# An mLSTM feeding a top-1 mixture of experts on one core: a new order of the work, a planner rule for the two engines that share a port, one product moved to VectorE, the odd row earlier, no explicit table load

## The chip, the cores and the metric

The kernel runs on one core of one Trainium2 chip. The time is device microseconds of one execution. The core has five engines that matter here: PE (TensorE), DVE (VectorE), ACT (ScalarE), POOL (GpSimd) and SP (SyncE, which here only issues DMAs). Each runs its own instructions strictly in order and waits on semaphores for the others.

## The reference, cut to what matters

Inputs are q, k, v and an output gate of 4 batches, 8 heads, 768 steps, 40 dimensions; two gates per step; 3072 tokens, each with one of two modalities; 8 experts with w1 320x1024 and w2 1024x320.

```python
for t in range(S):                                  # mLSTM, one state per batch and head
    m_new = np.maximum(f_gate[:, :, t] + m, i_gate[:, :, t])
    C = f_stab * C + i_stab * np.einsum('bhd,bhe->bhde', vt, kt)
    n = f_stab * n + i_stab * kt
    nq = np.einsum('bhd,bhd->bh', n, qt)
    y[:, :, t] = sigmoid(o_gate) * (C @ qt) / np.maximum(np.abs(nq), 1.0)
x = y.transpose(0, 2, 1, 3).reshape(B * S, H * D)   # 3072 tokens of 320
logits = x @ w_gate + modality_bias[modality_id]
e_idx = np.argmax(logits, axis=1)                   # one expert per token
out[mask] = gate_w[mask, None] * (np.maximum(x[mask] @ w1[e], 0.0) @ w2[e])
```

## The kernel before, in words

The function `still_arm` (from about line 1590) is the arm that runs; a general arm behind a branch is not taken here. It uses two properties of the input: the state of the mLSTM barely changes once the first 64 steps are in, and nearly every token goes to the one expert that its modality's bias prefers. So there are two experts, called A and B, and a token with another expert is "odd"; one such odd token is worked out apart.

**Stages.** The state of each batch is built from the first 64 steps (`state`, L1798). 3072 tokens are 24 chunks of 128, taken in pairs i = 0 to 11. For each chunk `light` (matmul at L1945) multiplies queries by the state into a PSUM bank Y (pair 1: H). For each pair `token_rows` (from L1948) makes rows out of it: the gated product `xr` on DVE (L1961), the normaliser `ab` (clamped at L1973, its reciprocal at L1974, 128x16), then the **normaliser's product** xr = xr * ab, 128x640, on POOL (L1976); ACT casts the upper half to float16 (`rows`, L1979) and DVE takes the lower half (L1624, two instructions). POOL scatters each chunk's rows to a DRAM buffer x_s by token position (L1997), so that all tokens of an expert lie together. Chunks 22 and 23 (the first 64 steps) come from exact sums (`special`, L2033).

**Tiles of the experts.** Fifteen tiles: k0 A0, k1 A1, k2 B0, k3 B1 with 128 tokens, then A2, B2, A3, B3, A4, B4, A5, B5, A6, B6 with 256, and B7 with 96. The first three don't go through DRAM: PE picks their rows with 0/1 matrices (`select`, PE at L2120, 15 matmuls per tile and 25 for tile 1; ACT copies the result to `xt` at L2123 and L2124). The others are read from x_s by two transposing DMAs (L2096) once their rows have been scattered. For each tile `logits` (L2133) checks the expert, and `expert` (L2176) does layer 1 on PE into a bank H (L2197, 8 matmuls for each of 8 blocks), hh = relu on ACT (L2202), the rounding rest hl on DVE (L2204), layer 2 on PE into a bank O (L2214, 24 matmuls for each half of 128 tokens), the scaling `ob` on ACT (L2221) and the scatter to the output on POOL (L2222). Weights come in pieces of 768 or 640 columns through seven staging buffers; ACT makes the upper half (w1h, w2h: L1903) and DVE the rest (w1l, w2l: L1904).

**The odd row** (`odd_row`, L2236 to 2285): DVE adds up which token is odd (`fpr`, `fs`, L2240 to 2244), PE sums over partitions (Y<-fs, L2246), DVE turns that into indices (L2247 to 2254), POOL gathers the row (`xrow`, L2256), SP reads a register (L2261) and loads that expert's weights into the staging and gate buffers (L2264, L2266). DVE makes `xf` (L2269, L2270), eight products (L2272), `fh` (L2274), one scaling (L2275) and seven multiply-adds into `facc` (L2277); PE sums over partitions (Y<-facc, L2280); ACT and POOL write it (L2282, L2283).

**What sets the order.** Nothing is issued directly. Each instruction becomes a task of `Plan` (L39 to 160) with its engine, an estimated duration, what it reads and writes, a bias, an optional start bound `nb` and an added latency `lat`. A task's due time `late` is its distance to the end along its dependences, and `plan.early` moves it earlier. `NUDGE` adds a number to the bias of single tasks by their count. A list scheduler plays the engines forward; among ready tasks it takes the smallest late + bias; the instructions are emitted in that order. Tasks marked `lk` on DVE and POOL are kept from overlapping in that play. Behind it, `idle_products` puts products with a zero matrix (M<-zw, O<-zw, L1731) where the play shows PE idle in its first 60 us, so that PE is not idle for long. The table load of ACT is asked for once at the beginning (L1724).

## Time and profile before

| what | value |
|---|---|
| median of 3 runs | 224.15 us (222.76 to 226.62) |
| the profiled execution | 222.62 us, of which 220.9 us are the span |
| PE busy in the span | 206.7 us (94%) |
| DVE, ACT, POOL busy | 142.1, 97.0, 86.1 us |
| granted TensorE clock | 0.992 |

Rows of a timeline read: start in us, duration in us, engine, line, operation, output <- inputs, shapes, count; in brackets the idle time of that engine just ahead and what ended it. Rows of a table by stage read: stretch, length, then busy time and number of instructions of PE, PE's weight loads, DVE, ACT and POOL, the granted clock, the DMA share and the GB/s moved. Rows of the waits read: the waiting engine and line, what it waited for, then us in total, times, longest.

### The profile page before, as it was taken

The numbers are of one execution on the slowest core, as the hardware profiler recorded it, in microseconds if no ns is written. First come the engines' busy times: TensorE is split into PE (matmuls) and PEld (weight loads), VectorE is DVE, ScalarE is ACT, GpSimd is POOL, SyncE is SP. The second block draws the span as 40 slices with busy tenths as digits, with TensorE's granted clock in tenths as the row PEclk, the third lists the DMA queues.
The fourth block names the chain that finished last, engine by engine and source line by source line (L and its number), as shares of the span: only waits on it lengthen the run. The fifth ranks groups of instructions, "written<-read, shape, count | busy, mean of one in ns | idle before, by whom it ended". The sixth has DMA issues, their size and how long they took to land.

```text
span 220.9 us, 5482 instructions
## 1 busy us (share of the span) xinstructions
PE 206.7 (94%) x2139; PEld 167.2 (76%) x2139; DVE 142.1 (64%) x421; ACT 97.0 (44%) x200; POOL 86.1 (39%) x98
## 2 busy tenths in 40 slices
PE   7987699999999999999999999999999999998960
PEld 2875589888887877878878768878878787785840
DVE  4789799998679463566386438425324858629960
ACT  2567688684255553342754313314553223143210
POOL 6458569421106716345048723526030120410321
PEclk9999999999999999999999999999999999999996
DMA  6989997989400659202774493202840010493100
GB/s 181 362 273 362 382 381 132 324 144 265 129 0 34 169 164 222 100 3 91 157 133 132 127 224 79 60 34 91 124 87 32 0 59 3 128 309 132 61 0 13
DMA packets 29783, 31.50 MB, mean 143 GB/s; under 512 B 21862, under 2 KB 22408, under 8 KB 29496
## 3 DMA queue, kind: packets, MB, share of 16 engines
q1 hardware_dynamic: 27176, 22.89, 38.9%
q0 software_dynamic: 2432, 8.13, 10.3%
q8 instruction: 18, 0.29, 0.6%
q14 instruction: 13, 0.11, 0.2%
q10 hardware_dynamic: 144, 0.07, 0.1%
HBM read 19.17 MB, written 8.43 MB: 125 GB/s over the span
## 4 chain that ended last, share of the span: by engine, by line
PE 68%; issue 14%; DMA 5%; POOL 2%; SPq 2%; DVE 2%; ACT 2%; another core or an unknown queue 1%; POOLq 1%; DVEq 0%
PE H L2197 32%; PE O L2214 28%; PE Y L1945 3%; DMA stage<-in_w1p 3%; DMA og<-in_ogl 3%; POOL out L2222 2%; PE M L2151 2%; SPq L1902 1%; PE Y L2043 1%; PE Y L2058 1%; POOLq L2407 1%; DVE hl L2204 1%; PE Y L1810 1%; PE O L2120 0%
## 5 line engine op out<-in xcount | busy, mean ns | idle before, releaser
L2204 DVE SCALAR_TENSOR_TENSOR hl<-H,hh 128x512 f16<-128x512 f32 (+1 forms) x50 | 33.9, 682 | 30.2 <-ACT hh L2202 25.6
L2214 PEld LDWEIGHTS <-hh 128*128 128x128 f16 (+1 forms) x400 | 38.6, 99 | 13.9 <-issue 0.5
L2202 ACT ACTIVATE hh<-H 128x512 f16<-128x512 f32 (+1 forms) x50 | 29.4, 592 | 42.1 <-PE H L2197 37.7
L2222 POOL DMA_INDIRECT out<-ob,ois x25 | 26.1, 1042 | 52.4 <-ACT ob L2221 35.9
L2197 PE MATMUL H<-xt,w1hB 128*128 128x256 f16 (+2 forms) x320 | 45.8, 251 | 0.1
L2197 PE MATMUL H<-xt,w1hA 128*128 128x256 f16 (+1 forms) x280 | 43.5, 257 | 0.3 <-issue 0.3
L2197 PE MATMUL H<-xt,w1lB 128*128 128x256 f16 (+2 forms) x192 | 40.6, 251 | 0.0
L2197 PE MATMUL H<-xt,w1lA 128*128 128x256 f16 (+1 forms) x168 | 37.9, 257 | 1.5 <-DVE w1lA L1904 1.5
L1976 POOL TENSOR_TENSOR xr<-xr,ab 128x640 f32<-128x640 f32 x12 | 17.1, 1424 | 38.9 <-DVE ab L1974 17.3
L2197 PEld LDWEIGHTS <-w1hB 128*128 128x128 f16 x320 | 28.5, 98 | 2.8
L1997 POOL DMA_INDIRECT x_s<-rows,pos_i x24 | 25.3, 1052 | 12.9 <-issue 7.0
L2214 PE MATMUL O<-w2hB,hh 128*128 128x320 f16 (+1 forms) x104 | 28.8, 299 | 0.0
L2214 PE MATMUL O<-w2lB,hh 128*128 128x320 f16 (+1 forms) x104 | 28.7, 299 | 0.0
L2197 PEld LDWEIGHTS <-w1hA 128*128 128x128 f16 x280 | 25.3, 98 | 3.3 <-issue 0.8
L2214 PE MATMUL O<-w2hA,hh 128*128 128x320 f16 x96 | 26.5, 299 | 0.0
L2214 PE MATMUL O<-w2lA,hh 128*128 128x320 f16 x96 | 26.5, 299 | 0.0
L2221 ACT ACTIVATE ob<-O,facs 128x320 f32<-128x320 f32 (+1 forms) x25 | 13.1, 526 | 30.6 <-PE O L2214 20.1
L2214 PEld LDWEIGHTS <-hl 128*128 128x128 f16 (+1 forms) x200 | 19.2, 99 | 8.7 <-DVE hl L2204 1.8
L2197 PEld LDWEIGHTS <-w1lB 128*128 128x128 f16 x192 | 18.7, 98 | 1.6 <-issue 0.3
L2197 PEld LDWEIGHTS <-w1lA 128*128 128x128 f16 x168 | 16.4, 98 | 3.1 <-DVE w1lA L1904 1.7
L2214 PE MATMUL O<-w2hB,hl 128*128 128x320 f16 (+1 forms) x104 | 17.1, 299 | 0.7 <-DVE hl L2204 0.7
L2214 PE MATMUL O<-w2hA,hl 128*128 128x320 f16 x96 | 15.3, 299 | 0.2 <-DVE hl L2204 0.2
(198 smaller groups left out, 294.0 us busy)
## 6 DMA issues: line engine op xcount, KB each, us to landing
qg<-in_ql SPq DMA_DIRECT2D x11, 384.0 KB
og<-in_ogl SPq DMA_DIRECT2D x12, 320.0 KB
...
```

The source lines that it names most:

```text
L1810: t_.matmul(u3[0:120, g], lhsT=kw[pr][rs, 3 * g:3 * g + 3].rearrange("p h d -> p (h d)"), rhs=kvs[pr][rs, 9 * D + HQ * g:9 * D + HQ * (g + ...
L1902: dma(n // 2, lambda sv=sv, src=src: sy.dma_start(sv, src()), r=[f"reg{c}"], w=[f"stage{k}"])
L1945: t_.matmul(y[p0:p1, HQ * g:HQ * g + w], lhsT=q[0:k, j, g, p0:p1], rhs=s[0:k, g, 0:w], start=(g == 0 and e == 0), stop=(g == 2 and e == n ...
L1976: lane((320 if lane is dve else 290) * n, lambda z=z, f=f, n=n: f(x4[:, z].rearrange("p c h d -> p (c h) d"), x4[:, z].rearrange("p c h d ...
L1997: ins = g_.indirect_dma_start(out=x_s[:, :], out_offset=bass.IndirectOffsetOnAxis(ap=pos_i[:, c:c + 1].bitcast(U32), axis=0), in_=rows[:, ...
L2151: t_.matmul(M0[:, 16 * h:16 * h + 16], lhsT=x[:, b], rhs=wgr[:, b % 3].rearrange("p a e -> p (a e)"), start=(h == 0 and b == 0), stop=(h = ...
L2197: t_.matmul(hp3[:, i], lhsT=l, rhs=r, start=(i == 0 and q == 0), stop=(i == g - 1 and q == 7), skip_group_check=True)
L2202: act(g * n, lambda fl=fl, hp3=hp3: s_.activation(hh[:, fl, 0:n], hp3, AF.Relu), r=[nb], w=[f"hh{j}{f}" for f in range(f0, f0 + g)])
L2204: dve(g * n, lambda fl=fl, hp3=hp3: v.scalar_tensor_tensor(hl[:, fl, 0:n], hp3, 0.0, hh[:, fl, 0:n], ALU.max, ALU.subtract), r=[nb] + [f"h ...
L2214: t_.matmul(op[0:z, 0:DM], lhsT=t[:, f, P * h:P * h + z], rhs=w[:, f], start=(i == 0), stop=(i == 23))
L2221: act(400, lambda h=h, op=op, o=o: s_.mul(obs[o][0:z], op[0:z, 0:DM], facs[0:z, s["q0"] + h:s["q0"] + h + 1]), r=[no, f"fac{k}"], w=[f"ob{ ...
L2222: swdma(164, lambda h=h, o=o: disjoint("outf", g_.indirect_dma_start(out=out[:, :], out_offset=bass.IndirectOffsetOnAxis(ap=ois[0:z, s["q0 ...
```

## The change

1. **The planner's rule for the shared port.** Before, a marked task on DVE or POOL starts, in the play, no sooner than the other's last marked task ends, less HOP (0.13). Now a marked POOL task starts LEAD (0.17) after DVE's. Eight small DVE operations are newly marked.
2. **The third pair's product on VectorE**: `BY_DVE` holds 4, so that for i = 2 the product xr = xr * ab (128x640) is one DVE instruction (L1629 in the new file) instead of a POOL one.
3. **The odd row sooner**: its tasks get 30 of earliness from end to end (`ODD`); before, those from `xf` to `facc` had none, and the rest 20. `SOON` is 30 for the other late tasks.
4. **No explicit table load**: the task that asked for it is gone, so all later tasks count one less.
5. **Costs in the play**: latency for the first loads of keys and gates, for the gather and for the last multiply-add; the absolute sums start later (`nb`).
6. **A new order**: the table `NUDGE` is another one, which together with 1 to 5 gives each engine another order.

```diff
 NUDGE = {
-    5: -33, 34: 162, 35: 57, 36: 44, 38: 34, 43: -8, 45: -116, 52: -7, 53: -123, 56: 240, 60: 266, 67: 11, 73: -1, 76: 8, 78: 12,
+    5: -33, 33: 453, 34: 199, 35: 44, 37: 34, 42: -8, 44: -116, 51: -7, 52: -123, 59: 122, 61: -11, 62: -19, 66: 11, 69: -23, 71:
...
     DMA_KB = 380.0
+    LEAD = 0.17
...
             if t["lk"]:
-                s = max(s, port["POOL" if name == "DVE" else "DVE"] - self.HOP)
+                s = max(s, port["POOL"] - self.HOP if name == "DVE" else port["DVE"] + self.LEAD)
...
-SOON = 20.0
+SOON = 30.0
 HINT = 12.0
+ODD = 30.0
 RING = 12
 BY_POOL = (3, 4)
-BY_DVE = ()
+BY_DVE = (4,)
...
-        dma(373, lambda: sy.dma_start(kvs[pr], ...), w=[f"kv{pr}"], bias=...)
+        dma(373, lambda: sy.dma_start(kvs[pr], ...), w=[f"kv{pr}"], lat=0.5 if pr == 0 else 0.0, bias=...)
-        dma(328, lambda: sy.dma_start(og[i % 4], ...), w=[f"og{i % 4}"], bias=...)
+        dma(328, lambda: sy.dma_start(og[i % 4], ...), w=[f"og{i % 4}"], lat=0.9 if i < 2 else 0.0, bias=...)
...
-    plan.add("ACT", 1.4, lambda: s_.preload_act_table_set("exp_and_others"), (), ["table"], bias=-90)
...
-    (ss, e_i, ssc, ss: four small DVE operations on the counts)
+    (the same four, with lk=True)
...
-            r=[f"rowh{c0}", f"rowh{c0 + 1}"], w=["sums"], bias=15, nb=45 if i < 4 else None)
+            r=[f"rowh{c0}", f"rowh{c0 + 1}"], w=["sums"], bias=15, nb=45 if i < 4 else 110)
...
-            dve(25, lambda i=i, t=t: v.tensor_tensor(fpr[:, 1 + i], fm, t, ALU.mult), r=fms + ks, w=["fpr"])
+            dve(25, lambda i=i, t=t: v.tensor_tensor(fpr[:, 1 + i], fm, t, ALU.mult), r=fms + ks, w=["fpr"], lk=True)
...
-            bounds_check=2 * CAP + P - 1, oob_is_err=False), NC), r=["fp_i"] + [f"xs{c}" for c in range(NC)], w=["xrow"])
+            bounds_check=2 * CAP + P - 1, oob_is_err=False), NC), r=["fp_i"] + [f"xs{c}" for c in range(NC)], w=["xrow"], lat=3.0)
...
-        plan.early = 0.0
         dve(64, lambda: v.tensor_tensor(xf[:, 256:DM], xrow[:, 256:DM], xrow[:, DM:384], ALU.add), r=["xrow"], w=["xf"], lk=True)
...
-            dve(320, lambda f=f: v.scalar_tensor_tensor(facc, ...), r=["og0", "fh"], w=["facc"], lk=True)
-        plan.early = SOON
+            dve(320, lambda f=f: v.scalar_tensor_tensor(facc, ...), r=["og0", "fh"], w=["facc"], lk=True, lat=2.5 if f == NFC - 1 else 0.0)
...
-        dve(24, lambda: v.tensor_tensor(okc, cum, lo_f, ALU.is_ge), r=["cum", "cst"], w=["okc"])
-        dve(24, lambda: v.tensor_tensor(ra, cum, hi_f, ALU.is_le), r=["cum", "cst"], w=["ra"])
+    (the same two, with lk=True)
...
                 check_sums()
+                plan.early = ODD
                 odd_row()
                 plan.early = SOON
```

Line numbers of the new file lie 3 to 5 above those of the old one in this part. Three places of the new order matter below. In the names, xr_169, xr_170 and xr_171 are the buffers of pairs 0, 1 and 2 (and later of 3, 4, 5), hh_110 and hl_110 and so on the buffers of the expert tiles.

**First place: DVE around the rows of pair 2**, at about 15 to 21 us. Before:

```order
L1973 TENSOR_SCALAR ab_167<-ab_167 128x16
L1974 RECIPROCAL ab_167<-ab_167 128x16
L1624 SCALAR_TENSOR_TENSOR rows<-xr_170,rows 128x2x64
L1624 SCALAR_TENSOR_TENSOR rows<-xr_170,rows 128x2x256
L2344 TENSOR_SCALAR wgr<-wg_sb 128x3x8
L1961 SCALAR_TENSOR_TENSOR xr_169<-og,Y_70 128x320
L1961 SCALAR_TENSOR_TENSOR xr_169<-og,Y_69 128x320
L1864 TENSOR_SCALAR ss<-cumx 128x2
L1870 TENSOR_TENSOR bias<-consts,ss 128x16
L1870 TENSOR_TENSOR bt<-consts,ss 128x16
L1873 TENSOR_TENSOR bias<-bias,bt 128x16
L2345 SCALAR_TENSOR_TENSOR wgr<-wg_sb,wgr 128x3x8
```

and after it w1lA (L1904, 128x768) and the two lower halves of pair 2. Of the change:

```order
L1629 SCALAR_TENSOR_TENSOR rows<-xr_170,rows 128x2x256
L1978 RECIPROCAL ab_167<-ab_167 128x16
L1629 SCALAR_TENSOR_TENSOR xr_171<-xr_171,ab_167 128x640
L1977 TENSOR_SCALAR ab_168<-ab_168 128x16
L1868 TENSOR_SCALAR ss<-cumx 128x2
L1874 TENSOR_TENSOR bt<-consts,ss 128x16
L1874 TENSOR_TENSOR bias<-consts,ss 128x16
L1877 TENSOR_TENSOR bias<-bias,bt 128x16
L1965 SCALAR_TENSOR_TENSOR xr_169<-og,Y_69 128x320
L1629 SCALAR_TENSOR_TENSOR rows<-xr_171,rows 128x2x64
L1629 SCALAR_TENSOR_TENSOR rows<-xr_171,rows 128x2x256
L1908 SCALAR_TENSOR_TENSOR w1lA<-stage,w1hA 128x3x256
```

The product (third row) is now DVE's own, behind pair 1's lower halves; the two lower halves of pair 2 stand ahead of the first w1lA, no longer behind it. POOL's queue has six scatters in a row there instead of one, the product, and five. On PE the last ten matmuls that pick tile 1 (those on pair 2's rows) stood behind 16 matmuls of tile 0's layer 1; now they stand ahead of them, and so does half of the `light` that stood behind the picking of tile 2.

**Second place: SP around the transposes of tile 6** (xt_101; tile 5's is xt_100, tile 7's xt_102). Before:

```order
L2096 DMA_TRANSPOSE xt_100<-x_s 128x5x256
L2102 DMA ids<-x_s 128x1 x2
L1715 DMA og<-in_ogl 128x640
L2014 DMA x_s<-zrow 128x656 x2
L1712 DMA qg_79<-in_ql 128x768
L1712 DMA qg_80<-in_ql 128x768
L2365 DMA gl<-in_gll 32x1536
L2102 DMA ids<-x_s 128x2x1
L1715 DMA og<-in_ogl 128x640 x2
L2096 DMA_TRANSPOSE xt_101<-x_s 128x5x256
L2096 DMA_TRANSPOSE xt_102<-x_s 128x5x256
```

Of the change:

```order
L2100 DMA_TRANSPOSE xt_100<-x_s 128x5x256
L1720 DMA og<-in_ogl 128x640
L1717 DMA qg_80<-in_ql 128x768
L2018 DMA x_s<-zrow 128x656 x2
L2367 DMA gl<-in_gll 32x1536
L2106 DMA ids<-x_s 128x2x1
L1717 DMA qg_78<-in_ql 128x768
L1720 DMA og<-in_ogl 128x640
L1717 DMA qg_79<-in_ql 128x768
L1720 DMA og<-in_ogl 128x640
L2106 DMA ids<-x_s 128x2x1
L2100 DMA_TRANSPOSE xt_101<-x_s 128x5x256
```

Three loads of gates (og) still stand ahead of tile 6's transposes, and one more load of queries (qg_78) and one of indices (ids) moved ahead of them.

**Third place: DVE at the odd row.** Before:

```order
L2204 SCALAR_TENSOR_TENSOR hl_113<-H_63,hh_111 128x512
L2291 TENSOR_TENSOR ra<-cumx,consts 128x24
L2272 SCALAR_TENSOR_TENSOR fjunk,fh<-stage,xf 128x320
L2204 SCALAR_TENSOR_TENSOR hl_113<-H_64,hh_111 128x512
L2272 SCALAR_TENSOR_TENSOR fjunk,fh<-stage,xf 128x320 x7
L2274 TENSOR_SCALAR fh<-fh,fl 128x8
L2275 TENSOR_SCALAR facc<-og,fh 128x320
L2277 SCALAR_TENSOR_TENSOR facc<-og,fh,facc 128x320 x5
L2204 SCALAR_TENSOR_TENSOR hl_112<-H_65,hh_110 128x4x96
L2277 SCALAR_TENSOR_TENSOR facc<-og,fh,facc 128x320 x2
L2204 SCALAR_TENSOR_TENSOR hl_112<-H_63,hh_110 128x4x96
```

Here hl_113 is tile B6 and hl_112 the last tile, B7. Of the change, with hl_112 of tile A6 in the first four rows:

```order
L2208 SCALAR_TENSOR_TENSOR hl_112<-H_63,hh_110 128x512
L2208 SCALAR_TENSOR_TENSOR hl_112<-H_64,hh_110 128x512
L2208 SCALAR_TENSOR_TENSOR hl_112<-H_65,hh_110 128x512
L2208 SCALAR_TENSOR_TENSOR hl_112<-H_63,hh_110 128x512
L2272 TENSOR_TENSOR xf<-xrow 128x64
L2273 TENSOR_TENSOR xf<-xrow 128x256
L2275 SCALAR_TENSOR_TENSOR fjunk,fh<-stage,xf 128x320 x8
L2277 TENSOR_SCALAR fh<-fh,fl 128x8
L2278 TENSOR_SCALAR facc<-og,fh 128x320
L2280 SCALAR_TENSOR_TENSOR facc<-og,fh,facc 128x320 x5
L2208 SCALAR_TENSOR_TENSOR hl_113<-H_64,hh_111 128x512
L2292 TENSOR_TENSOR okc<-cumx,consts 128x24
```

The whole odd row stands one tile of 256 tokens sooner. On PE, Y<-fs now comes ahead of tile A6 instead of inside A6's second layer, and Y<-facc comes eight layer 2 matmuls into B6 instead of twelve into the last tile.

16 lines of the change are left out of this document (9 added, 7 removed), and 25 rows, old and new, of the table NUDGE.

## The prediction, as it was put on record

> **What bounds the kernel now.** I read the page's first two lines, then a table by stage, PE's waits, and the timelines of the places where PE waits.
>
> ```profile
> span 220.9 us, 5482 instructions
> PE 206.7 (94%) x2139; PEld 167.2 (76%) x2139; DVE 142.1 (64%) x421; ACT 97.0 (44%) x200; POOL 86.1 (39%) x98
> 10.00:20.00 10.00, 8.64 (x92) 7.22 (x92) 9.08 (x27) 6.99 (x19) 6.01 (x8) 1.00 0.96 311
> 20.00:26.00 6.00, 3.37 (x43) 2.53 (x44) 4.69 (x8) 3.66 (x8) 4.78 (x5) 1.00 1.03 399
> 26.00:200.00 174.00, 173.39 (x1821) 142.89 (x1818) 109.49 (x308) 79.43 (x162) 65.43 (x61) 1.00 0.49 131
> 200.00:220.90 20.90, 12.91 (x134) 9.52 (x132) 13.16 (x46) 3.05 (x7) 3.90 (x4) 0.91 0.09 30
> ```
>
> Between 26 and 200 PE idles 0.61 us (174.00 less 173.39). The clock is full there. What the change can gain lies ahead of 26, where PE also runs fillers, and behind 200; between them it can only lose. PE's waits say the same, one of the front and one of the tail (two more stand in brackets in the timelines below):
>
> ```profile
> PE H L2197 <- DVE w1lA L1904: 1.5, 1, 1.5
> PE O L2214 <- DVE hl L2204: 0.9, 2, 0.7
> ```
>  PE's matmuls of use are the same number in both kernels; only fillers differ, by one or two, all ahead of 23 us by the order.
>
> **The change, part one: the front.** What came in what order:
>
> ```profile
> 14.23 1.44 DVE L1624 SCALAR_TENSOR_TENSOR rows<-xr,rows 128x128 f16<-128x128 f32 x2
> 15.95 0.82 DVE L1624 SCALAR_TENSOR_TENSOR rows<-xr,rows 128x128 f16<-128x128 f32 x2
> 17.57 1.67 DVE L1864 TENSOR_SCALAR ss<-cumx 128x2 f32<-128x2 f32 x1
> 19.80 0.95 DVE L1904 SCALAR_TENSOR_TENSOR w1lA<-stage,w1hA 128x768 f16<-128x768 f32 x1
> 20.67 0.89 DVE L1624 SCALAR_TENSOR_TENSOR rows<-xr,rows 128x128 f16<-128x128 f32 x2
> 23.81 0.82 DVE L1904 SCALAR_TENSOR_TENSOR w2lA<-stage,w2hA 128x640 f16<-128x640 f32 x1
> 13.65 1.26 POOL L1976 TENSOR_TENSOR xr<-xr,ab 128x640 f32<-128x640 f32 x1 [0.18 <-DVE ab L1974]
> 17.93 1.28 POOL L1976 TENSOR_TENSOR xr<-xr,ab 128x640 f32<-128x640 f32 x1
> 19.24 0.72 ACT L1979 CAST rows<-xr 128x640 f16<-128x640 f32 x1 [1.19 <-POOL xr L1976]
> 24.41 0.27 ACT L2124 CAST xt<-O 128x128 f16<-128x128 f32 x1 [2.18 <-remote]
> 21.60 0.72 PE L2120 MATMUL O<-sel,rows 128*128 128x128 f16 x10
> 25.22 1.01 PE L2120 MATMUL O<-sel,rows 128*128 128x128 f16 x15 [1.82 <-ACT xt L2123]
> 26.07 1.52 PE L1945 MATMUL Y<-S,qg 120*128 120x123 f32 x12
> ```
>
> Pair 2's product ran on POOL and ended at 17.93 + 1.28 = 19.21. Two engines hung on it. ACT cast from 19.24. And DVE's tiny `ss` (two columns) took from 17.57 to 19.24, so it stood still under POOL's product: a stall of about 1.5 us, which then pushed w1lA (PE waited 1.5 for it) and pair 2's lower halves (20.67 to 21.56). Behind them ten picking matmuls, ACT's copy of tile 1, and PE at 25.22.
>
> [...]
>
> The moved product on DVE isn't in the trace. Its nearest row is a two-input product of the same 128x640, w2lA at 0.82. Below it stands 0.69 for 512 columns (an hl, quoted in the next part), above it POOL's own 1.28; I take 0.82, the same size on the same engine. At 1.28 everything up to tile 2's picks comes 0.46 later, at 0.69 0.13 sooner. It is placed behind pair 1's lower halves (15.95 + 0.82 = 16.77, and 0.25 for the reciprocal), so xr is done at about 17.8 instead of 19.21. ACT casts behind the copy of tile 0: done 18.5 instead of 19.96. DVE meanwhile does the small operations without the stall and a gate product, and the lower halves end at 20.0 instead of 21.56. w1lA follows and ends at about 20.95 instead of 20.75: it pays for the halves' going first, but PE now has the picking of tile 1 to do in that time. PE: ten picks at 20.4 to 21.1, 16 layer 1 matmuls to 22.0, then it waits for ACT, whose queue has four weight casts (0.84 each) ahead of tile 1's copy. These fit between 18.5 and 22.3, the copy ends at 23.0, and PE picks tile 2 at 23.05 instead of 25.22: −2.17.
>
> One piece I can't explain: ACT's copy started at 24.41 although the tenth pick ended at 21.60 + 0.72 = 22.32; the view names a remote event. If that 2.1 comes back, the gain there is what moved ahead of it, 1.1. I take the middle, −1.6. Six of the twelve `light` matmuls at 26.07 go into PE's idle time before it: 1.52 / 2 = −0.75. **Front: −2.35**, bounds −2.9 and 0 (the end where transfers decide, below).
>
> **Part two: the tail.**
>
> ```profile
> 188.18 0.28 PE L2246 MATMUL Y<-fs,ones_f 128*128 128x5 f32 x2
> 198.24 0.23 DVE L2269 TENSOR_TENSOR xf<-xrow 128x64 f32<-128x64 f16 x1 [2.85 <-DMA xrow<-x_s,fp_i]
> 202.31 0.69 DVE L2204 SCALAR_TENSOR_TENSOR hl<-H,hh 128x512 f16<-128x512 f32 x1
> 202.91 0.48 DVE L2272 SCALAR_TENSOR_TENSOR fjunk<-stage,xf 128x320 f32<-128x320 f32 x1
> 206.65 0.23 DVE L2274 TENSOR_SCALAR fh<-fh,fl 128x8 f32<-128x8 f32 x1
> 207.34 2.90 DVE L2277 SCALAR_TENSOR_TENSOR facc<-og,fh,facc 128x320 f32<-128x320 f32 x5
> 203.05 0.45 PE L2214 MATMUL O<-w2hB,hl 128*128 128x320 f16 x2 [0.66 <-DVE hl L2204]
> 211.81 0.70 PE L2280 MATMUL Y<-facc,ones_f 128*2 128x320 f32 x2 [0.70 <-DVE facc L2277]
> 150.55 7.00 PE H L2197 x64
> 157.56 6.52 PE O L2214 x48
> 215.16 0.94 POOL L2222 DMA_INDIRECT out<-ob,ois  x1 [0.99 <-ACT ob L2221]
> ```
>
> DVE waits 2.85 for the gathered row with tile B6's hl queued behind `xf`; PE lacks them twice (0.9 in all by the waits). The sum facc is then late by 0.70 in the last tile. The new order puts Y<-fs one tile further ahead. Behind it lie now A6 and B6 (7.00 + 6.52 each), B7 at 96 of 256 columns for layer 1 (about 2.6) and 3.3 of layer 2: some 33 us of PE, where 23.4 lay behind it before (211.8 − 188.2 and the last 12). So the odd row has 9.7 us more. Counting from T0 = Y<-fs: the row is there at +10.1 (188.18 to 198.24); A6's four hl are ahead of it in DVE's queue, so nothing of A6 is held by the gather; then xf 0.6, eight products 4.3 (seven took 3.74, from 202.91 to 206.65), 0.7 for fh and scaling, five multiply-adds 2.9: B6's first hl is done at about +19.1. PE needs the bank that this hl reads for its fourth block of B6, at 7.00 + 6.52 + three quarters of 7.00 = +18.8 to +19, so 0 to 0.3 is lost there. facc is done at +20.2; PE asks for it behind B6's layer 1 and eight matmuls (1.1) at 7.00 + 6.52 + 7.00 + 1.1 + 0.3 = +21.9. So 0.9 + 0.7 go and 0.2 comes: **−1.4**. Bounds: −1.7 with all of it, and +1.0 if the DVE burst (9 us without a hole for hl) makes PE wait at B6's hl.
>
> **Part three: the table load.**
>
> ```profile
> 198.18 1.28 ACT L1724 ACT_TABLE_LOAD   x1
> 199.47 0.60 ACT L2202 ACTIVATE hh<-H 128x512 f16<-128x512 f32 x1
> ```
>
> The trace has one load there, in the tail, though it was asked for at the beginning. The hh behind it waits 1.3, but the hl on that chain stands behind DVE's wait for the row anyhow, and PE's loss is already counted in the 0.9. Without the task, the load may come at another place; if it is on the path it costs 1.28, and is inside the bounds of the tail. **0**. [...]
>
> **Part four: everything moved.** From 26 to 200 the old order loses 0.61. The new one is new everywhere there, and the same dependences with other slack tend to open a hole or two of 0.4 to 0.8: I take **+0.9** over the old, with 0 and +3 as bounds. The planner's rule itself changes only the order, and its price is in this term.
>
> Sum: −2.35 − 1.4 + 0 + 0.9 = −2.85 against the profiled execution's 222.62 (span 220.9 and 1.7 around it): 219.8. That execution is 1.5 below the median of the runs, 224.15; since I can't tell which the next runs will be like, I add half of it: **220.5**.
>
> **The rivals.**
>
> A, *all of it is kept*: no remote event, no new hole: −2.17 − 0.75 − 1.7 − 0.8 (old small holes gone too) = −5.4, 217.2, with the half offset 218. For it: the first two parts touch separate engines' waits. Against it: 0.61 in 174 us is already little.
>
> B, *transfers bound the front*, so that waiting moves and doesn't go (two timeline rows, and one of the chain of waits):
>
> ```profile
> 21.38 0.84 ACT L1903 ACTIVATE w1hA<-stage 128x768 f16<-128x768 f32 x1 [0.16 <-DMA stage<-in_w1p]
> 41.18 0.95 DVE L1904 SCALAR_TENSOR_TENSOR w1lB<-stage,w1hB 128x768 f16<-128x768 f32 x1
> 40.86 3.57 PE H L2197 x64
> ```
>
> The DMA share is 0.96 and 1.03 from 10 to 30 us, with 311 to 399 GB/s, ACT waits for a stage of weights at 21.38, the last w1lB ends at 42.13 while PE is already in B's first block from 40.86. If PE comes there 2.35 sooner and the weights don't, it waits 2.35: then only tail and holes are left, −1.4 + 0.9 = −0.5, 222.1, with the half offset 222.9. Against it: the new order puts the four w1B loads and w1lB further ahead.
>
> C, *slower: SP's queue holds the transposes of tile 6*:
>
> ```profile
> SPq L1715 <- ACT gjunk L1912: 47.7, 5, 20.5
> 79.64 2.83 SPq L2096 DMA_TRANSPOSE xt<-x_s  x2
> ```
>
> SP waited 47.7 us in five holds at loads of gates, for ACT's junk pass over the old ones, the longest 20.5, with everything behind it in SP's queue, the transposes of tiles 6 and 7 among it. Tile 6's went out from 79.64; with 4 that I allow for issue and flight they are there some 17.5 behind the last `light` that they need. By the new order PE has about 19.9 us of other work between that `light` and tile 6's logits (a layer 1 of 7.00, 72 layer 2 matmuls at 6.52 / 48 each, and `light`s), so 2.4 of slack. One load of queries and one of indices more now stand ahead. If a gate load is held 7 longer than before, PE waits 4.6: 219.8 + 4.6 = 224.4, with the offset 225.1, and 226 where tile 7 follows. It decides from a hold 2.4 longer. Against it: the number of gate loads ahead of these transposes is the same.
>
> That the change doesn't do what it says is open for the rule: DVE's small operations could still land under a POOL product elsewhere, since POOL's real durations differ from the plan's. That costs DVE 1.3 at a time, and PE nothing where it has 0.5 us of queue; it is in the +0.9.
>
> **How the numbers follow.** The forecast case (219 to 222.5) gets 0.50, A 0.20, B 0.17, C 0.13. About 2% can be told from no change here, 4.5 us: faster is below 219.7, slower above 228.6. A counts as faster, and 0.15 of the forecast's 0.50; the far end of C (0.06), where more tiles follow, as slower. Together faster 0.35, same 0.59, slower 0.06. The range leaves out a tenth on each side: from 216.8 (A's 217.2 less a little) to 224.9 (B whole, and most of C out).
>
> **What would show it.** Right: `ss` at 0.16 us, the product at 0.8 on DVE near 17, PE at tile 2's picks before 24.2, PE idle from 26 to 200 under 2 us, no wait of DVE's `xf` longer than 0.5 with an hl queued, no wait of PE for facc. Wrong: a PE wait over 1.5 for x of tile 6 or 7 (C), for w1lB (B), or a first pick of tile 2 not earlier than 25 with the remote event again.

## The result, and the profile after

The changed kernel takes 226.11 us (median of 22 runs, 224.14 to 232.28), the kernel before 225.16 (22 runs, 222.76 to 228.31). The ratio is 1.0086 with a 95% interval of 1.0057 to 1.0115: about 0.9% slower, where −1.6% was forecast, and above the range's upper end of 224.9. The profiled execution of the change (the first profile, in what follows) took 226.87 us. That of before (222.62) lies at the fast end of its kernel's times, so the 4.2 us between the two profiles overstate the difference. It is about 1 us between the medians and 1.9 by the ratio, which compares only the fast runs of both kernels.

After's table by stage, with the cuts of before's and one more at 80 to 104 us. Columns: stretch and its length, busy time (and count) of PE, PEld, DVE, ACT, POOL, then the granted clock, the DMA share and GB/s:

```profile
span 225.2 us, 5485 instructions
PE 209.4 (93%) x2141; PEld 168.5 (75%) x2141; DVE 140.3 (62%) x422; ACT 95.6 (42%) x199; POOL 83.0 (37%) x97
10.00:20.00 10.00, 9.09 (x94) 7.58 (x95) 8.35 (x26) 7.03 (x20) 5.04 (x6) 1.00 0.90 291
20.00:26.00 6.00, 4.32 (x52) 3.13 (x51) 4.50 (x9) 4.75 (x8) 4.54 (x4) 1.00 1.00 385
26.00:80.00 54.00, 53.37 (x629) 45.41 (x630) 45.18 (x112) 32.96 (x67) 22.38 (x21) 1.00 0.65 197
80.00:104.00 24.00, 20.14 (x193) 15.08 (x191) 13.53 (x41) 7.71 (x18) 10.28 (x10) 0.93 0.47 112
104.00:200.00 96.00, 95.68 (x942) 77.52 (x940) 54.12 (x176) 34.24 (x73) 30.92 (x30) 1.00 0.40 101
```

The same stretch of before:

```profile
80.00:104.00 24.00, 24.00 (x236) 19.17 (x234) 14.70 (x44) 9.89 (x20) 11.27 (x10) 1.00 0.47 108
```

The front did get better: between 10 and 26 us PE is busy 13.41 us instead of 12.01, fillers counted. But between 80 and 104 it loses 3.86 us that before did not lose, and its clock falls to 0.93 of full there as well. Both kernels have the same 2091 matmuls of use, so I set the two traces side by side by how much of that work was done. After is some 0.6 us ahead at 33 to 43 us, 2.1 behind at 84, 6.0 behind at 104, 5.8 behind at 185 to 200, and 4.1 behind at the end. The two orders do different work at different times, so single figures swing by 1 to 3 us without any loss; they tell a loss only between stretches where they stand still, here 33 to 43 and 185 to 200. The loss is made in two places, near 82 and near 98; chip 13 below gives its size free of the orders.

What PE waited for there, from the list of waits (total, times, longest) and from the chain of waits (start, duration, step):

```profile
PE H L2201 <- issue: 2.6, 4, 1.2
PE Y L1949 <- issue: 1.0, 2, 0.6
```

```profile
97.59 0.85 issue
98.44 0.49 PE H L2201 x3
98.93 1.20 issue
```

"Issue" means that PE waited for nothing that the profile shows: by the profile its next matmul was free to go, and it did not go. ACT at the same moments, and POOL ahead of them (timelines):

```profile
83.19 0.60 ACT L2206 ACTIVATE hh<-H 128x512 f16<-128x512 f32 x1 [4.18 <-remote]
```

```profile
91.23 1.05 POOL L2001 DMA_INDIRECT x_s<-rows,pos_i  x1 [1.52 <-ACT rows L1983]
92.59 0.97 POOL L2001 DMA_INDIRECT x_s<-rows,pos_i  x1 [0.30 <-DVE lg L2163]
93.86 0.98 POOL L2001 DMA_INDIRECT x_s<-rows,pos_i  x1 [0.30 <-ACT ex L2167]
95.14 0.97 POOL L2001 DMA_INDIRECT x_s<-rows,pos_i  x1 [0.30 <-issue]
96.42 0.97 POOL L2226 DMA_INDIRECT out<-ob,ois  x1 [0.30 <-issue]
97.70 0.97 POOL L2226 DMA_INDIRECT out<-ob,ois  x1 [0.30 <-issue]
```

ACT's hh waits 4.18 for a "remote" event, though only matmuls of this core fill its bank. The trace has the end of each matmul and the moment at which PE's semaphore for it changes; nearly everywhere the two lie within 0.35 us of each other. Worked out from these records, the places in the body where they lie 1.0 or more apart, with what POOL's timeline has there:

```
kernel   POOL's DMAs in a row     matmul ended   semaphore    late
before   five, 19.4 to 26.0       22.32          24.39        2.1
before   five, 71.7 to 77.8       74.77          75.94        1.2
before   three, 100.9 to 104.5   104.07         105.20        1.1
before   five, 117.5 to 123.7    123.58         124.61        1.0
after    six, 17.2 to 25.5        21.17          24.58        3.4
after    six, 74.0 to 81.6        80.14          83.17        3.0
after    six, 91.2 to 98.7        96.61         100.18        3.6
```

I call this a **hold**: PE's semaphores come 1 to 4 us late, and meanwhile PE issues in pieces. No semaphore of DVE, ACT or POOL is over 0.35 late there. Each hold stands within or at the end of a series of indirect DMAs that POOL issues some 1.28 us apart with nothing between. The new order lets four scatters of x run into the two of an output tile, twice; before's series in the middle have five at most and its holds there stay near 1 us. That the series is the cause was so far only a reading of where the holds stand.

The front and the tail, step by step. DVE and PE in the front (timelines):

```profile
14.32 1.90 DVE L1629 SCALAR_TENSOR_TENSOR rows<-xr,rows 128x128 f16<-128x128 f32 x2
16.26 0.90 DVE L1629 SCALAR_TENSOR_TENSOR rows<-xr,rows 128x128 f16<-128x128 f32 x2
17.35 0.82 DVE L1629 SCALAR_TENSOR_TENSOR xr<-xr,ab 128x640 f32<-128x640 f32 x1
18.17 0.26 DVE L1868 TENSOR_SCALAR ss<-cumx 128x2 f32<-128x2 f32 x1
19.27 0.88 DVE L1629 SCALAR_TENSOR_TENSOR rows<-xr,rows 128x128 f16<-128x128 f32 x2
```

```profile
22.20 1.03 PE L1735 MATMUL M<-zw 128*128 128x512 f16 x4
24.53 1.17 PE L2124 MATMUL O<-sel,rows 128*128 128x128 f16 x15 [1.30 <-issue]
```

The product takes 0.82 us on DVE, `ss` 0.26 instead of 1.67, and the lower halves end at 20.15, all as forecast. Tile 2's picks start at 24.53, not at 23.05. They wait for ACT's copy of tile 1 (23.89 to 24.48). Of these 1.48 us about 1.0 comes from ACT's four weight casts, which end at 23.35 instead of 22.3, with 1.01 of idle time ahead of them and between them. The other 0.53 is once more a hold: ACT waits that long for a "remote" event. In the tail:

```profile
193.63 0.23 DVE L2272 TENSOR_TENSOR xf<-xrow 128x64 f32<-128x64 f16 x1 [0.67 <-DMA xrow<-x_s,fp_i]
199.19 2.90 DVE L2280 SCALAR_TENSOR_TENSOR facc<-og,fh,facc 128x320 f32<-128x320 f32 x5
202.01 0.68 DVE L2208 SCALAR_TENSOR_TENSOR hl<-H,hh 128x512 f16<-128x512 f32 x1
206.12 0.70 PE L2282 MATMUL Y<-facc,ones_f 128*2 128x320 f32 x2
```

The row is waited for 0.67 instead of 2.85, PE waits for neither hl nor facc, and from 200 us to the end after wins back 1.8 us.

### The profile page after: what moved, and what is told of

Its sections match the earlier page's. It is cut to its first block, busy times and chain, and to the rows that moved or that the text cites. A ratio compares the mean times of both kernels' runs of the same rounds, so it can differ in the third digit from the quotient of the medians.

```text
span 225.2 us, 5485 instructions
## 1 busy us (share of the span) xinstructions
PE 209.4 (93%) x2141; PEld 168.5 (75%) x2141; DVE 140.3 (62%) x422; ACT 95.6 (42%) x199; POOL 83.0 (37%) x97
## 4 chain that ended last, share of the span: by engine, by line
PE 54%; issue 13%; DVE 11%; DMA 8%; POOL 6%; another core or an unknown queue 2%; SPq 2%; ACT 1%; POOLq 0%; DVEq 0%; ACTq 0%
PE H L2201 23%; PE O L2218 22%; DMA xrow<-x_s,fp_i 3%; DMA x_s<-rows,pos_i 3%; PE Y L1949 3%; DVE fjunk L2275 2%; PE O L1735 2%; DVE facc L2280 2%; DMA og<-in_ogl 2%; POOL x_s L2001 2%; DVE xr L1965 1%; POOL rows L1986 1%; DVE rows L1629 1%; SPq L2100 1%
## 5 line engine op out<-in xcount | busy, mean ns | idle before, releaser
L2218 PEld LDWEIGHTS <-hh 128*128 128x128 f16 (+1 forms) x400 | 39.1, 101 | 15.7 <-issue 0.8
L2226 POOL DMA_INDIRECT out<-ob,ois x25 | 24.6, 984 | 63.9 <-ACT ob L2225 33.4
L2001 POOL DMA_INDIRECT x_s<-rows,pos_i x24 | 26.2, 1090 | 16.0 <-ACT ob L2225 4.6
L2218 PE MATMUL O<-w2hA,hh 128*128 128x320 f16 x96 | 27.9, 311 | 0.0
L2218 PE MATMUL O<-w2lA,hh 128*128 128x320 f16 x96 | 27.7, 310 | 0.0
L1980 POOL TENSOR_TENSOR xr<-xr,ab 128x640 f32<-128x640 f32 x11 | 14.4, 1310 | 35.1 <-DVE ab L1978 22.4
L2218 PE MATMUL O<-w2hB,hl 128*128 128x320 f16 (+1 forms) x104 | 16.6, 299 | 0.0
```

Of the source, the lines that this page charges most:

```text
L1980: lane((320 if lane is dve else 290) * n, lambda z=z, f=f, n=n: f(x4[:, z].rearrange("p c h d -> p (c h) d"), x4[:, z].rearrange("p c h d ...
L2001: ins = g_.indirect_dma_start(out=x_s[:, :], out_offset=bass.IndirectOffsetOnAxis(ap=pos_i[:, c:c + 1].bitcast(U32), axis=0), in_=rows[:, ...
L2218: t_.matmul(op[0:z, 0:DM], lhsT=t[:, f, P * h:P * h + z], rhs=w[:, f], start=(i == 0), stop=(i == 23))
L2226: swdma(164, lambda h=h, o=o: disjoint("outf", g_.indirect_dma_start(out=out[:, :], out_offset=bass.IndirectOffsetOnAxis(ap=ois[0:z, s["q0 ...
```

## The experiments

Two theories stood at the start. **Series**: POOL's unbroken series of indirect DMAs hold PE, and the new order has longer ones. **Dependences**: the new order makes PE wait for data in the ordinary way, and the records near 82 and 98 only look odd. Later questions were whether the cause is the data that the scatters move or their posting, and what else the new order costs. "Ratio" is always to the kernel before on the same chip, with its 95% interval. Holds turned out to go with the chip: all eight traces of chips 6 and 8 have late semaphores of PE (over 1 us), none of the ten of chips 13 and 14 has any over 0.6 us. So each group names its chip. The expectations use short names of their own for the theories; what each run decides is said here in words.

### Chip 6: both kernels again, pauses in the series, a series added

after_again and before_again are the two kernels as they stand.

> The changed kernel as it is, looked at once more. Theory P (a long unbroken series of POOL's indirect DMAs holds PE up and delays its semaphore updates): PE loses 2 to 6 us again between 80 and 104 us, at the ends of the same two series of six. Theory R (the holds are chance, different in each execution): the loss is elsewhere or missing, and the span is 220 to 222.

> The kernel before as it is, looked at once more. Theory P: no hold of PE over 1.5 us, only the short ones at the ends of series of three to five indirect DMAs, 0.5 to 1.2 us of late semaphore each, near 74, 78, 104 and 124 us. Theory R: holds of 1 to 4 us at other places.

after_again took 224.34 us (one run), before_again 222.2 (one run; the kernel before has a median of 225.21 over 11 runs on this chip); single runs don't tell which is faster here. The holds are at the same places: after 21.57→24.15, 80.51→82.97 and 96.42→99.61, before 22.45→24.50, 74.88→76.03, 104.17→105.32. They belong to the orders and aren't an accident of one execution.

after_paused puts two fills of a spare tile, about 1.3 us together, on POOL behind six of the scatters of the two middle series:

```
+    pause = tl([P, 640], F32, "pause")
+    PAUSE = {'xs11': 2, 'xs12': 2, 'out4.0': 2, 'xs15': 2, 'xs17': 2, 'out5.0': 2}
...
                 plan.tasks[i]["fn"]()
+                for _ in range(PAUSE.get(plan.tasks[i].get("tag"), 0)):
+                    g_.memset(pause, 0.0)
```

> The changed kernel with pauses of about 1.3 us (two memsets of a spare tile) on POOL inside the two series of six indirect DMAs. Theory P: PE's loss between 80 and 104 us falls under 1 us, the clock stays full there, and the time is 2 to 5 us below the changed kernel's, 221 to 223. Theory R: no difference beyond 0.5 us. Theory T (it is the issue of the transposing DMAs on SP that holds PE, which fell together with the series): PE still loses 1 us or more while the two transposes of tiles 6 and 8 are issued, and the time stays within 1 us.

Measured: 222.42 us (220.4 to 225.73), ratio 0.9887 [0.9819, 0.9955]. The stretch from 80 to 104 us, of after_again and then of after_paused:

```profile
80.00:104.00 24.00, 21.09 (x217) 16.42 (x216) 13.54 (x41) 8.24 (x20) 10.64 (x10) 1.00 0.60 118
```

```profile
80.00:104.00 24.00, 24.00 (x251) 19.80 (x249) 15.83 (x50) 10.54 (x23) 20.07 (x25) 1.00 0.46 119
```

POOL does about twice the work (20.07 against 10.64), the same scatters among it, and PE has no hole at all. The latest semaphore there is 0.7 us late; the hold of the front, which got no pause, is still there (23.43→27.39). Were the holes waits for data, more work on POOL could not have taken them away. The expectation's third theory, the transposes that SP issues near the ends of the series (80.72 and 97.88 in after), falls as well: they are issued at 86.35 and 101.65 here and PE loses nothing.

before_burst adds six scatters of rows to a spare buffer in the kernel before, at a place where it had no hold (behind `out10.0`, 163 us):

```
+    def more():
+        for c in range(6):
+            ins = g_.indirect_dma_start(
+                out=spare[:, :], out_offset=bass.IndirectOffsetOnAxis(ap=pos_i[:, c:c + 1].bitcast(U32), axis=0),
+                in_=rows[:, c], in_offset=None, bounds_check=NX - 1, oob_is_err=False)
+            disjoint("spare", ins)
...
+                if plan.tasks[i].get("tag") == "out10.0":
+                    more()
```

> The kernel before with six more indirect DMAs on POOL, one behind the other, that write rows to a spare DRAM buffer at about 166 to 174 us, where no transposes are issued and PE waits for nothing. Theory P: PE's semaphore updates are late by 1 us or more near the end of the series, PE loses 1 to 4 us there, the time is 1 to 5 us above the kernel before. Theories R and T: PE loses nothing there, the time is the same within 0.5 us.

Measured: 230.34 us (229.09 to 232.54), ratio 1.0301 [1.0215, 1.0388]. A row of ACT's timeline, and the stretch where the series ends; then the first ten of these microseconds in before:

```profile
172.12 0.60 ACT L2203 ACTIVATE hh<-H 128x512 f16<-128x512 f32 x1 [5.34 <-remote]
```

```profile
166.00:176.00 10.00, 7.21 (x50) 5.20 (x48) 3.47 (x13) 1.90 (x4) 4.86 (x5) 0.82 0.28 103
176.00:186.00 10.00, 10.00 (x76) 7.17 (x74) 5.96 (x17) 1.87 (x4) 1.65 (x2) 0.84 0.04 16
```

```profile
166.00:176.00 10.00, 10.00 (x93) 8.18 (x92) 6.09 (x19) 3.13 (x6) 0.33 (x1) 1.00 0.05 18
```

With the scatters on either side POOL now has eight in a row, 162.2 to 172.1. They make a hold where none was: a semaphore 3.8 us late (168.33→172.10), PE idle 2.79, and the granted clock at 0.82 and 0.84 over 20 us, some 6 us in all where 1 to 4 were expected (2.79, and 0.18 and 0.16 of the two stretches; by work done PE falls 6.3 behind before_again between 165 and 175). No instruction uses what the six move. This shows that a series on POOL does it, on this chip.

### Chip 8: posting or data; the product put back; the odd row put back

before_burst_void is before_burst with indices beyond the bound, so that the six DMAs are posted and move nothing:

```
+    void_f, void_i = small([1], "void_f"), small([1], "void_i", I32)
+    v.memset(void_f, float(2 * NX))
+    v.tensor_copy(void_i, void_f)
...
-                out=spare[:, :], out_offset=bass.IndirectOffsetOnAxis(ap=pos_i[:, c:c + 1].bitcast(U32), axis=0),
+                out=spare[:, :], out_offset=bass.IndirectOffsetOnAxis(ap=void_i.bitcast(U32), axis=0),
```

> The kernel before with the same six further indirect DMAs at about 166 to 174 us, but every index out of range, so that no row is moved. Theory P1 (the holds come from the data that the series moves): no hold of PE, time as before within 0.5 us. Theory P2 (they come from POOL making and posting the DMAs, whatever is moved): PE's semaphores late by 1 to 4 us near the end of the series and 3 us or more lost, as with the moving series.

Measured: 227.64 us (226.75 to 228.52), ratio 1.0206 [1.0152, 1.026].

```profile
166.00:176.00 10.00, 7.21 (x50) 5.14 (x48) 3.17 (x12) 1.90 (x4) 4.64 (x5) 0.80 0.07 19
176.00:186.00 10.00, 10.00 (x78) 7.24 (x77) 5.96 (x17) 1.87 (x4) 2.09 (x2) 0.86 0.04 16
```

The transfers fall from 103 to 19 GB/s (before has 18 there), and the hold is the same to 0.1 us (168.11→171.82, 3.7 late; PE idle 2.79). The moved data isn't the cause; posting is enough.

after_product_back puts the third pair's product back on POOL, in the new order:

```
-            lane, f = (dve, tt) if 2 * i + hs[0] in BY_DVE else (pool, g_.tensor_tensor)
+            lane, f = (dve, g_.tensor_tensor) if 2 * i + hs[0] in BY_DVE else (pool, g_.tensor_tensor)
```

> The changed kernel with pair 2's product put back on POOL at the same place of the order; nothing else differs. Theory of the prediction: POOL's product and the stall of ss on VectorE come back (ss about 1.5 us long), the picking of tile 2 starts 1 to 2 us later, and the time rises by 1 to 2 us. Rival: the hold of PE behind the front's six indirect DMAs already sets the start of tile 2 (24.5 us), so the product's place gives nothing: within 0.5 us of the changed kernel.

Measured: 227.81 us (226.71 to 232.42), ratio 1.0204 [1.015, 1.0257]. DVE (timeline):

```profile
17.61 2.26 DVE L1874 TENSOR_TENSOR bias<-consts,ss 128x16 f32<-128x16 f32 x1
20.61 0.89 DVE L1629 SCALAR_TENSOR_TENSOR rows<-xr,rows 128x128 f16<-128x128 f32 x2
```

A small operation is held up again, 2.26 us where after took 0.17 for the same line. It ends 0.05 behind POOL's product (18.55 to 19.82), though it began 0.94 ahead of it; why it stood that early isn't shown. The lower halves end 1.35 later than in after (21.50 against 20.15). So the edit does what it says. The order on PE is the same as in after_again, so the two can be set side by side exactly: PE is 1.2 us behind at 24 and 0.3 at 28 to 36, which is what the rival expected of the front, and 2.6 to 3.1 from 40 on. Most is not lost in the front: tile 3's rows come later, its transposes go out on SP at 33.00 instead of 30.81, and PE then waits 3.4 in all for hh, most of it at 38 to 48 us. The run after_paused_front takes that up.

after_odd_late leaves the new order but lets the odd row's work from `xf` on come at before's place:

```
+        plan.early = 0.0
         dve(64, lambda: v.tensor_tensor(xf[:, 256:DM], xrow[:, 256:DM], xrow[:, DM:384], ALU.add), r=["xrow"], w=["xf"], lk=True)
...
+        plan.early = 20.0
         n2, y2 = take("Y")
...
-                plan.early = ODD
+                plan.early = 20.0
                 odd_row()
```

> The changed kernel with the odd row's earliness as it was (20, and none from xf to facc); the order is the same up to about 150 us. The tail theory: waits of PE for hl and facc of 1 to 2 us come back behind 195 us, and the time rises by 1.2 to 1.8 us over the changed kernel. Rival: the odd row was hidden enough in either order: within 0.5 us.

Measured: 225.42 us (224.27 to 227.56), ratio 1.0136 [1.0074, 1.0198].

```profile
197.99 0.23 DVE L2273 TENSOR_TENSOR xf<-xrow 128x64 f32<-128x64 f16 x1 [7.54 <-DMA xrow<-x_s,fp_i]
199.00 0.69 DVE L2208 SCALAR_TENSOR_TENSOR hl<-H,hh 128x512 f16<-128x512 f32 x1
```

`xf` stands 24.7 us ahead of the span's end instead of 31.5 in after, 6.8 later, and DVE waits 7.54 for the row. Yet PE waits for nothing in the tail and ends level with after_again (0.06 apart at equal work). One hl stands behind the wait, B6's first, whose hh ends at 197.81 on ACT: it is 1.2 us late and PE has other work for that long. In before the hl behind `xf` had its hh at 196.41 and came at 199.44, with the next two crowded behind it. The tail's gain is therefore not due to how early the row's work comes. Two differences are left: where that work falls among the hl, and two absolute sums of 0.81 us each (L1990) that before has right behind `xf` and between two hl (198.72 and 200.04), while after and after_odd_late have their last one at 152 to 155. No run parts these two. The time (1.0136, where the change itself had 1.0086 in its own runs) says little here: the two intervals overlap, and the change wasn't run on this chip.

after_paused_front adds pauses in the front's series:

```
-    PAUSE = {'xs11': 2, 'xs12': 2, 'out4.0': 2, 'xs15': 2, 'xs17': 2, 'out5.0': 2}
+    PAUSE = {'xs11': 2, 'xs12': 2, 'out4.0': 2, 'xs15': 2, 'xs17': 2, 'out5.0': 2, 'xs1': 2, 'xs3': 2}
```

> The changed kernel with the pauses in the two series of six, and two more pauses in the front's series of six (after its second and fourth DMA). Theory P: PE's semaphores are late by under 1 us in the front too, the picking of tile 2 starts at about 23 instead of 24.5 us, and the time falls by a further 0.5 to 1.5 us below the paused kernel's. Rival: the pauses make tile 3's rows late, or the weights set the front, and nothing or less than nothing is gained.

Measured: 223.86 us (222.37 to 225.09), ratio 1.0026 [0.9993, 1.0059]. At 26 to 30 us it is 1.9 us further than after_again, and then it loses all of it. PE's wait, ACT and SP there:

```profile
PE O L2219 <- ACT hh L2207: 3.4, 1, 3.4
```

```profile
39.24 0.74 ACT L1907 ACTIVATE w2hB<-stage 128x640 f16<-128x640 f32 x1 [4.19 <-DMA stage<-in_w]
32.87 1.36 SPq L2101 DMA_TRANSPOSE xt<-x_s  x1
34.98 0.95 SPq L1906 DMA_DIRECT2D stage<-in_w  x2
```

ACT waits 4.19 for a load of B's second-layer weights, with hh queued behind, and PE for hh. The load stands on SP behind tile 3's transposes, which wait for tile 3's scattered rows; pauses ahead of those scatters make it worse. Before had issued seven of its eight loads of w2 pieces ahead of these transposes, the change five. This is a second cost of the new order, independent of holds, but not a steady one: in the first profile PE waits for nothing there. So the rival of this run came true.

### Chip 14: the load ahead of the transposes; which chip

In after_paused_later and after_paused_front_later tile 3's transposes go behind the two loads in SP's queue (the **swap**); the rest is after_paused and after_paused_front:

```
+    p = next(n for n, i in enumerate(order) if plan.tasks[i].get("tag") == "tr3")
+    q = [n for n, i in enumerate(order) if n > p and plan.tasks[i]["eng"] == "SP" and plan.tasks[i]["w"] and plan.tasks[i]["w"][0].startswith("stage")][1]
+    moved = order[p]
...
+    order[p:q + 1] = order[p + 1:q + 1] + [moved]
```

> The changed kernel with the pauses in the two series of six, and in SP's queue the transposes of tile 3 put behind the two loads of B's second-layer weights that stood behind them. Queue theory (ACT's upper half of w2B, with hh queued behind it, is late because its load stands behind transposes that wait for rows): ACT's wait for that stage (0.6 us and more near 36) goes, PE's hole near 44 goes, and the time falls 0.3 to 1 us below the paused kernel's. Rival: the transposes of tile 3 are then late for its logits, and nothing is gained.

> The same, with the front's pauses too. Queue theory: the wait of PE for hh at 37 to 40 us (3.4 us with the front's pauses alone) goes, the front's gain of 1.9 us at 30 us is kept, and the time is 219 to 221 us, the lowest here. Rival (the transfers themselves are the bound, not their order): the wait stays at 2 us or more in another place.

Measured: 220.44 us, 0.9942 [0.9908, 0.9977], and 220.59 us, 0.995 [0.9916, 0.9984]. No wait for hh is left in either. With the pauses in the front PE waits instead for the transposes that were moved back, as that run's rival said (a wait in another place):

```profile
PE M L2157 <- DMA xt<-x_s: 1.8, 1, 1.8
```

before_paused puts pauses into before's own series, before_burst3 adds three scatters instead of six:

```
+    PAUSE = {'xs3': 2, 'xs5': 2, 'xs11': 2, 'xs13': 2, 'xs17': 2, 'xs18': 2, 'xs20': 2}
```

```
-        for c in range(6):
+        for c in range(3):
```

> The kernel before with pauses of the same length inside its own series of four to six indirect DMAs (front, 72 to 78, 101 to 104 and 117 to 123 us). Theory P: its short holds (0.5 to 2 us of late semaphores) go, but PE hardly waited for them: 0 to 1 us is gained, or up to 2 lost where the pauses in the front hold tile 3's rows. If instead it gains 2 us or more, the paused change is no better than the paused kernel before, and the change's other parts bring nothing.

> The kernel before with three further indirect DMAs at about 166 to 170 us instead of six. If the hold grows with the length of the unbroken series beyond some four, PE loses under 1.5 us; if each DMA costs its share, about half of the six's 6.7 us, 3 us.

Measured: 223.66 us, 1.006 [1.0018, 1.0103], and 221.87 us, 0.9989 [0.9955, 1.0023]. Both were meant to show how the hold goes with the length of a series, and neither does, for no execution traced on this chip has a hold, not even in the front. What they show is the price of pauses where there is nothing to mend, 0.6%. So the two kernels and the six scatters were run unchanged on this chip:

> The changed kernel as it is, on one more chip. If this chip shows the holds (late semaphores of PE at the ends of POOL's series): 2 to 4 us lost between 80 and 104 us and a time 0.5 to 1.5% above the kernel before. If it doesn't, as the last one: nothing lost there, and the time 0.5 to 1% below the kernel before, since the front and the tail are then what is left.

> The kernel before as it is, on the same chip as the run beside it. With the holds: semaphores of PE late by 0.5 to 2 us near 22, 75, 78, 104 and 124 us. Without: none over 0.3 us.

> The kernel before with the six further indirect DMAs, on the same chip. With the holds: 6 to 7 us lost at 166 to 178 us, as the first time. Without: under 0.5 us lost, which would say that the hold belongs to the chip or to how it is recorded, and not to the six DMAs alone.

Measured: after_c 222.23 us, ratio 0.9998 [0.9963, 1.0032]; before_c 222.25 and before_burst_c 221.37 (one run each; before's median is 221.53 here). The stretches of before_burst_c, which on chip 6 lost some 6 us:

```profile
166.00:176.00 10.00, 10.00 (x93) 8.01 (x91) 6.53 (x17) 2.54 (x5) 4.99 (x5) 1.00 0.24 86
176.00:186.00 10.00, 10.00 (x101) 8.49 (x99) 7.54 (x36) 3.23 (x7) 1.12 (x2) 1.00 0.09 34
```

The same scatters, on POOL for the same time (4.99 against 4.86), cost nothing here. No semaphore of PE is over 0.6 us late in the three executions. The change was expected 0.5 to 1% below before on such a chip and is level with it. after_c has instead the wait for hh in full, and one thing more, an early wait for queries:

```profile
PE O L2218 <- ACT hh L2206: 3.4, 2, 3.1
PE Y L1949 <- DMA qg<-in_ql: 1.9, 1, 1.9
```

```profile
40.80 0.74 ACT L1907 ACTIVATE w2hB<-stage 128x640 f16<-128x640 f32 x1 [3.67 <-DMA stage<-in_w]
```

### Chip 13: the swap in SP's queue alone

after_later is after with the swap and without pauses; after_d is after unchanged, after_paused_later_d is after_paused_later again.

> The changed kernel with one thing changed: in SP's queue tile 3's transposes stand behind the two loads of B's second-layer weights, not ahead of them; no pauses. Queue theory: the hole of PE near 38 to 42 us (3.4 us in the last look at the changed kernel) is under 0.7 us, and the time lies 0.5 to 1.5% below the changed kernel's on the same chip. Rival (the hole came from the disturbed clock of that one execution): the same as the changed kernel within 0.3%.

> The changed kernel as it is, beside the run above on the same chip. Queue theory: a hole of 1 to 3.5 us for hh near 38 to 45 us, the time within 0.5% of the kernel before where the chip has no holds, 0.5 to 1.3% above it where it has. Rival: no such hole, under 0.5 us.

> Both remedies again, on the same chip as the two above. Where the chip has no holds the pauses do nothing: the same as the first of these three within 0.3%. Where it has them: 1.5 to 2% below the first.

Measured: after_later 219.72 us, ratio 0.9905 [0.9876, 0.9934]; after_d 221.6 us, 0.995 [0.991, 0.999]; after_paused_later_d 220.53 us, 0.9949 [0.9919, 0.9978]. SP in after_later:

```profile
26.18 3.82 SPq L1906 DMA_DIRECT2D stage<-in_w  x3
31.15 1.33 SPq L2101 DMA_TRANSPOSE xt<-x_s  x1
```

Three loads go out ahead of the transposes, and the wait for hh near 37 to 40 us (0.8 in after_d, a little under the 1 to 3.5 expected) is gone; PE waits 0.7 for tile 3's transposes instead. By time the swap's worth isn't settled: 0.9905 and 0.995 lie 0.45% apart, just under the 0.5 to 1.5% expected, and their intervals overlap. The same swap with the pauses came out at 0.9949, so the two were not the same within 0.3% as expected. Pauses bring nothing on a chip without holds and may cost 0.4 to 0.6% (before_paused 1.006). The swap wasn't run on a chip with holds.

after_later and after_d give the holds' price as well. PE, DVE, ACT and POOL issue the same work in the same order in after, after_again, after_d and after_later (only SP differs, by the swap), so here equal work compares like with like. How far the two executions with holds are behind after_later, in us:

```
at (us)        80    82    86    95    98   104   110   200
after         0.4   0.4   2.6   2.6   3.3   6.9   7.0   7.4
after_again   0.8   0.9   2.5   2.4   3.0   4.4   4.4   4.8
```

Between 80 and 110 us the two holds cost 6.6 us in the first profile (2.2 and 4.4) and 3.6 in after_again (1.6 and 2.0); behind them it is 0.4 in either. And without holds the body of the new order loses nothing much against before's: set beside before_c, after_d goes from 1.1 behind at 30 to 36 us to 1.2 behind at 190 to 200, after_later from 1.0 ahead to 1.4 ahead. These are single executions.

The front can be compared in the same way. Tile 2's picks start at 25.22 in before and 24.53 in after, both with a hold; without one, they start at 23.95 in before_c and here in after_later:

```profile
23.05 1.01 PE L2126 MATMUL O<-sel,rows 128*128 128x128 f16 x15
```

after_d also shows the early wait again, and what follows it. Of after_d, and then of after_later, two stretches of the front:

```profile
9.00:11.00 2.00, 0.37 (x5) 0.19 (x3) 1.33 (x6) 2.00 (x8) 0.00 (x0) 1.00 1.07 396
11.00:15.00 4.00, 3.93 (x22) 3.88 (x23) 1.24 (x4) 1.31 (x6) 1.55 (x3) 0.57 0.61 202
```

```profile
9.00:11.00 2.00, 1.22 (x12) 1.07 (x12) 1.65 (x7) 1.86 (x7) 0.30 (x1) 1.00 1.08 388
11.00:15.00 4.00, 3.75 (x43) 3.24 (x43) 2.70 (x7) 2.17 (x7) 2.31 (x4) 1.00 0.73 211
```

Where a load of queries keeps PE waiting 1.70 us, PE stands for most of 9 to 11 us, its clock is then granted at 0.57, and half the matmuls are done in the next 4 us (22 against 43). Four of the twelve traced executions of after and its variants have it, none of the eight of before and its variants. They are those of after_c, after_d, after_paused and after_paused_later_d, which took 224.73, 222.01, 224.51 and 221.96 us where their medians are 222.23, 221.6, 222.42 and 220.53.

## Why the prediction failed, point by point

**The step that failed is part four, "everything moved", +0.9 with 3 as its upper bound.** In the first profile that term is about +6.5 (from some 0.6 ahead near 40 us to 5.8 behind at 185 to 200), in after_again against before_again +4.4. Holds make nearly all of it: against the same order on a chip without them, 6.6 and 3.6 are lost between 80 and 110 us, and without holds the term is 0.1 (after_d) or −0.4 (after_later) against before_c. So the part that I had reckoned with, holes of the ordinary kind, was smaller than the 0.9. I took the old order's stretch of 26 to 200 us, with its 0.61 of idle, as a sample of how orders behave, and asked only for ordinary waits. The cost came from something that the profile of before showed in one row and that I noted and left: ACT's copy at 24.41 behind "a remote event", 2.1 us after its matmul had ended. It was the hold of the front's series. I used it only as an end of the front's bounds. It is the only "remote" row of before; the small holds near 75, 104 and 124 show only where the end of a matmul is set beside its semaphore. Had I done that and asked what POOL did ahead of each, the question put to the new order would have been how long its series on POOL are. The order listing answers that: twice four scatters of x and then two of the output, with no product between.

**Part one, the front: −2.35 forecast, some 0.6 gained in the profile.** The steps on DVE came as worked out: the product 0.82, `ss` 0.26, lower halves by 20.15 (forecast 20.0). ACT's cast ended at 18.93 (forecast 18.5), its four weight casts 1.0 late. The −2.17 for tile 2's picks set a before with a hold against a change without one: without holds the picks do start at 23.05, the forecast's figure, but before_c's come sooner too, at 23.95. Like with like, and in single executions, they gain 0.7 (25.22 to 24.53, both with a hold) or 0.9, not the 1.1 to 2.17 from which I took the middle. The semaphores of the front were 3.4 late instead of 2.1, but only 0.53 of that held tile 2. And after_product_back, with the product on POOL, is only 0.3 behind at 28 to 36 us: where the product runs decides little of the front. That run shows the stall again on POOL's turn (2.26). The rows of the lower halves are longer beside a product of POOL too: in after 1.90 for the two at 14.32, which met the one from 14.20 to 15.46, and 0.90 for the two at 16.26; in before 1.44 and 0.82. That the two engines share a port is said only in the name of the planner's rule: no run shows what they share, only these times.

**Part two, the tail: −1.4 forecast, 1.8 gained from 200 us on** (1.4 in after_d and in after_later against before_c). The holes that were to close, 0.66 and 0.70, closed. The forecast had 0.9 for the first; the other 0.2 of that row is a wait at 127.93 us, in the body, so the sum came near partly by luck. The 0 to 0.2 that I charged for B6's hl did not come: its first starts at 202.01, behind the multiply-adds, and PE does not wait for it. But I ascribed the gain to the row's being sooner, and after_odd_late, with it 6.8 us later, has the same end. What counts is that the hl behind `xf` are not late when PE asks for them; whether the row's place among the hl or the absolute sums' being elsewhere does that is open.

**Part three, the table load: 0.** After has one load, at 1.25 us, and the tail has none; nothing waits for it. Before has that one too, at 1.26, so the load in the tail was the one that the task asked for. It held the hh behind it by some 0.2 us and not by 1.3: the three hh ahead of it start 1.75 apart, and this one starts 1.91 behind the third.

**The rivals.** A (all kept) did not happen, nor did B as told (a wait for w1lB); but loads do move the front in another place: in after_paused_later, without holds, ACT waits 2.1 us for pieces of w1A and tile 2's picks start at 25.19. C, SP's queue, had the right queue and the wrong place: tile 6's transposes held nothing up. Tile 3's did, by nothing in the first profile, 0.6 in after_d and 3.1 in after_c. I had looked at the loads ahead of the transposes and not at those that the order had moved behind them. Of the signs that I named, `ss` (0.26 instead of 0.16) and the product came as said, and so did PE's freedom from facc; `xf` waited 0.67 instead of at most 0.5. "Picks before 24.2" and "under 2 us from 26 to 200" failed, the latter by 3.86 us of idle in 24 us alone; and the remote event came back, at 24.5 instead of 25.

**What stays open.** Shown, on chips 6 and 8: a series makes the hold (3.8 us late in before_burst), breaking it removes it (at most 0.7 at 80 to 104 us in after_paused), and its data is not needed (3.7 late in before_burst_void). Whether it happens at all went with the chip in all 18 traces of the experiments. But the two chips with holds were used first and the two without later, so a change over time isn't ruled out. Not shown: through what PE's semaphores are kept back while those of other engines pass, why chips 6 and 8 have it and 13 and 14 don't, and from which length on. Three scatters instead of six were run only on a chip without holds, so the length isn't settled by experiment, and the five, three and six of the table are at different places. Each timed run on record lists its span and granted clock and so was recorded like the profiled ones; whether the kernel has holds when nothing is recorded stays open too. On a chip without holds the change by itself gives 0.5% or nothing (0.995 and 0.9998), so 1.6% would have been missed there too. The wait for hh and the early clock stand in the profiles of those chips. The swap in SP's queue takes away the first; what that is worth in time is not settled (0.9905 against 0.995, with overlapping intervals).
